# Late-token flag read two slots earlier, the common arm laid behind its branch, and the last slots of a mixture of experts reordered

## The chip, the core and the metric

The kernel runs on one core of a Trainium2 chip. The metric is the device time of one execution in microseconds. Of the kernel before, three runs took 663.84, 665.45 and 667.47 us (median 665.45). The profile comes from one further execution, of 667.0 us.

The core has five engines, each with its own queue of instructions, worked off in order: TensorE (PE, matmuls into PSUM; PEld is its weight load, listed apart), VectorE (DVE), ScalarE (ACT), GpSimd (POOL) and SyncE (SP, which here only issues DMAs). They wait for each other through semaphores.

## The reference

Three layers over 4 batches of 544 rows (32 global and 512 local) of 512 features, all in fp32:

```
x = attention(q_l, k_l, v_l, q_g, k_g, v_g)            # (4, 544, 512)
# layer 2: one expert of 8 for each row
logits = x @ w_gate; local = sigmoid(x @ w_local)
for s in rows of a batch:
    e = argmax(logits[s]) if s == 0 or local[s] < 0.5 else previous e
    y[s] = softmax(logits[s])[e] * (relu(x[s] @ w1[e]) @ w2[e])
# layer 3
h = relu(y @ w_in)
out = (h * sigmoid(conv3(h, conv_w))) @ w_out          # conv3 over the rows of a batch
```

The expert of a row depends on the data. `w_in`, `conv_w` and `w_out` of layer 3 arrive as 64-bit floats and are converted by integer operations on the chip.

## The kernel before, in words

**Products.** Each fp32 product is made of three matmuls in the type fp32r: every operand is split into a high part (a cast) and a low part (operand minus high part), and hi*hi, hi*lo and lo*hi are added up in PSUM. A weight's split is one ScalarE cast (`wh`, L1020) and one VectorE subtraction (`wl`, L1021).

**Slots.** Layer 2 gathers rows of one expert into slots of 128. Slots 0 and 1 are filled from the first rows while attention still runs. From slot 2 on (`Moe.run`, L1163) a `step` per slot goes through one straight line of code: first product of slot s (`l1`, 24 matmuls into `hp`), relu, transposes of the next slot's rows (`xs` to `xh`, `xl`), second product of slot s-1 (`l2`, 24 matmuls into `yp`), copy of `yp` to `ys` and scatter to `y_dram` by GpSimd, transposes of slot s's hidden rows (`hs` to `gh`, `gl`). So PE always has one product of each of two neighbouring slots. The straight line holds 22 slots, 0 to 21. Three more can be needed for other data; they stand in a conditional arm, the late arm.

**Weights of an expert.** W1 and W2 have one staging buffer each (`ws`). Where a slot has another expert than the one before, its splits run in a conditional arm on ScalarE and VectorE (`resplit`, L1268): W1's in the step before the slot, W2's at the end of the slot's own step.

**Beside the slots.** In steps 3 to 18 a chunk of `w_in` or `w_out` is loaded raw and converted (`conv64`, L983): six VectorE operations, one GpSimd addition, and a closing VectorE operation that is called in the next step. `wf` is their target. The conv weights (`cw6` to `cwr`, 24 x 128) are converted in the same way after step 19. `conv_w` (L1157) transposes `cwr` on PE and copies it to `cw`.

**Late tokens.** Layer 3 begins with batch 0. `late_tokens` (L924) marks whether a row of batch 0 sits in the last slot, and `late_flag` (L936) adds this mark, by a one-column matmul, to the test whether the late arm's slots are in use. All engines load the result from `esi` into a register and branch on it (L1172, L1173). If it is zero, nothing of the arm is done.

**The last slot, 21** (`last`, L1186): two of its four k parts of the first product, slot 20's second product, the other two parts with the conv weights and the flag among them, transposes, and its own second product. In that one lie layer 3's first pieces: the first batch's rows are loaded (`load0`), scaled by their gates one at a time (`scale0`), transposed (`xt0`, into `f_x0h`, `f_x0l`), and W1 is replaced by the split `w_in` (`split`). PREP0 lists what stands behind which k.

**Layer 3** (`Ffn2`) goes over 32 units of batch and feature block: 24 matmuls of 272 columns into `f1`, relu, three taps (one on ScalarE, two on VectorE), sigmoid, gate, split; then the second product. `w_out` is split at its beginning, on ScalarE and VectorE.

The program is recorded by hand: on each engine the instructions stand in the order in which the code calls them. At a conditional, an engine without instructions in an arm passes over it; an arm that isn't taken has a short partner that sets the semaphores to the values that the arm would have left.

Of the kernel before, what the change touches and what calls it, by code (L numbers as in the profile page):

```python
# [17 lines left out]
P = 128  # L18
# [6 lines left out]
NT = 17  # L25
# [940 lines left out]
SPLIT_W2 = {33: (0, 1), 34: (2, 3), 35: (4, 5), 36: (6, 7)}  # L966
FILL = {1: 1, 3: 1, 6: 3, 7: 1, 8: 3, 9: 1, 10: 1, 11: 1, 12: 2, 13: 3, 15: 5, 16: 8}
HALF = 5
K_LAST = 2
N_GLOB = 6  # L970
N_GS = 4
G_DVE = 1
N_Y = 24
SC_DVE = (0, 1, 2, 3)
PREP_F = ((3, 4, 5, 6), (1, 3, 5, 6), (1, 3, 5, 6))
PREP0 = {0: (0, 1, 12, 13), 3: (5, 2), 4: (6, 3), 5: (7, 4), 6: (8,), 7: (9,)}
POOL_L = ()
POOL_F = ()
DVE_F = (1, 3, 5, 7)
POOL_K = {1: (), 2: ()}  # L980


def conv64(nc, raw, out):  # L983
# [13 lines left out]
class Weights:  # L997
# [24 lines left out]

    def split(self, n, src, eng=None):
        for k in range(len(self.t[n])):
            self.split_k(n, src, k, eng or (self.nc.gpsimd if k in POOL_K[n] else self.nc.vector))


class Moe:
# [134 lines left out]
    def run(self, cw6, cwr, cw, f2):  # L1163
        nc, W, tc = self.nc, self.W, self.tc
        n = NSLOT - 3
        self.f2 = f2
        for s in range(NA, n - 1):
            self.step(s)
            if s == NA + 17:
                self.conv.append(conv64(nc, cw6, cwr))  # L1170
        self.last(n - 1, cwr, cw)
        r = nc.values_load(self.rt.esi[0:1, 4, 1:2], min_val=0, max_val=P + 1)  # L1172
        with tc.If(r != 0):  # L1173
            r = nc.values_load(self.rt.esi[0:1, 4, 0:1], min_val=0, max_val=NB)
            with tc.If(r > n - NA):
                for s in range(n, NSLOT):
                    self.slot(s)
                W.split(1, W.f)
            f2.load0()
            for i in range(5):  # L1180
                f2.scale0(i, self.ps)
                f2.xt0(i, self.ps)
        for k in range(NFC):
            W.split_k(2, W.f, k, nc.gpsimd if k in POOL_F else nc.vector, nc.vector if k in DVE_F else None)

    def last(self, s, cwr, cw):  # L1186
        nc, W, f2 = self.nc, self.W, self.f2
        hp, hs = self.h_tile(), self.tp.tile([P, FF], F32, tag="hs", name="hs")
        xt, ht = self.xt.pop(s), {}
        w, y = W.t[1], {}  # L1190
        ht = tuple(self.tp.tile([P, NFC, P], F32R, tag="g" + x, name="g" + x) for x in "hl")

        def split(a, b):
            for k in range(a, b):
                W.split_k(1, W.f, k, nc.gpsimd if k in POOL_K[1] else nc.vector)

        def resplit(a, b):
            with self.tc.If(self.chg[s] != 0):
                for k in range(a, b):
                    W.split_k(2, W.s, k, nc.gpsimd if k in POOL_L else nc.vector)  # L1200

        for k in range(K_LAST):
            self.l1_mm(xt, w, hp, k, range(2))
        split(0, K_LAST)
        nc.scalar.activation(self.sig, self.sig, AF.Sigmoid)
        self.out(s - 1, self.l2(self.ht.pop(s - 1), W.t[2]))
        f2.load0()
        resplit(0, 4)
        for k in range(K_LAST, NKC - 1):
            self.l1_mm(xt, w, hp, k, range(2))  # L1210
        self.conv_w(cwr, cw)
        self.rt.late_flag(s + 1, self.ps.tile([P, 4, P], F32, tag="tr", name="lf")[0:1, 0, 0:1])
        t = []
        for c in range(2):
            self.l1_mm(xt, w, hp, NKC - 1, (c,))
            self.relu_c(hp, hs, c)
        for a in (0, 4):
            t.append(self.hi_t(hs, ht, a, self.ps))
        for a in (0, 4):
            self.lo_t(ht, a, t[a // 4])  # L1220
        resplit(4, NFC)
        yp = self.y_tile()
        for k in range(NFC):
            self.l2_mm(ht, W.t[2], yp, k)
            for f in PREP0.get(k, ()):
                if f < 10:
                    (f2.scale0 if f < 5 else f2.xt0)(f % 5, self.ps)
                else:
                    split(f - 10, f - 9)
        self.out(s, yp)  # L1230

    def slot(self, s):
        nc, W = self.nc, self.W
# [37 lines left out]
        with self.tc.If(self.chg[s] != 0):  # L1271
            self.W.split(n, self.W.s, eng)

    def step(self, s):
        W, hi = self.W, NSLOT - 3
        if NA < s <= NA + 16:
            self.raw_load(s - NA - 1)
        hs = self.relu(self.l1(self.xt.pop(s), W.t[1]))
        if s + 3 < hi:
            self.xs[s + 3] = self.gather(s + 3)  # L1280
        self.xt[s + 1] = self.hi_lo_t(self.xs.pop(s + 1), NKC, "x")
        while self.conv:
            self.conv.pop()()
        self.resplit(s + 1, 1)
        if s + 2 < hi:
            self.fetch(s + 1, 1)
        if s == NA:
            for _ in self.rest:
                pass
        else:  # L1290
            self.out(s - 1, self.l2(self.ht.pop(s - 1), W.t[2]))
        self.ht[s] = self.hi_lo_t(hs, NFC, "g")
        self.resplit(s, 2)
        self.fetch(s, 2)
        if NA < s <= NA + 16:
            self.convert(s - NA - 1)
# [15 lines left out]
class Ffn2:  # L1312
# [14 lines left out]
    def part0(self, i):  # L1327
        return (SG, 0, GT, 4) if i == 0 else (P, SG + P * i - P, i - 1, i - 1)

    def scale0(self, i, ps):  # L1330
        n, _, j, a = self.part0(i)
        x = self.x_in[a][0:n]
        self.nc.vector.tensor_scalar(x, x, self.gate[0:n, j:j + 1], None, ALU.mult)
# [227 lines left out]
def moe_kernel(ctx, tc, q_l, k_l, v_l, q_g, k_g, v_g, w_gate, w_local, w1, w2, w_in, conv_w, w_out, out):  # L1561
    nc = tc.nc
    outf = out.rearrange("b s d -> (b s) d")
    with tc.manual_schedule():
# [95 lines left out]
        with ExitStack() as c2:  # L1660
# [15 lines left out]
            m.xt[NA] = m.hi_lo_t(m.xs.pop(NA), NKC, "x")  # L1676
            m.fetch(NA, 1)
            rt.gates()
            rt.late_tokens(NSLOT - 4)
        xa.close()  # L1680
        W.ffn(moe_ctx.enter_context(tc.tile_pool(name="w_f", bufs=1)))
        m.run(cw6, cwr, cw, f2)
# [34 lines left out]
```

## Time and profile before

| | |
|---|---|
| median of three runs | 665.45 us |
| profiled execution | 667.0 us, span 665.2 us, mean granted PE clock 0.968 |
| PE busy | 617.4 us (93%), 5898 matmuls |
| PEld busy | 517.8 us (78%) |
| VectorE busy | 421.7 us (63%) |
| ScalarE busy | 331.8 us (50%) |
| GpSimd busy | 199.0 us (30%) |

Times in the views are us from the span's start. Layer 2's straight line reaches from about 190 to 453 us, layer 3 from 457 us to the end. A timeline row gives start, duration from the first start to the last end of the merged instructions, engine, line of the code, operation, target and sources, shapes and count, and in brackets the idle time of the engine just before, with what ended it. Matmuls are pipelined: the distance from one start to the next tells their rate, the duration doesn't. [...] A queue's own instructions (loads of registers, branches, semaphores) have a "q" behind the engine's name; PE's stand under PEldq.

### The profile page before, as it was taken

What the parts mean: (1) busy time and instruction counts of PE and PEld (TensorE: products, weight loads), DVE (VectorE), ACT (ScalarE), POOL (GpSimd) and SP (SyncE); (2) the same over time, 40 slices, a digit from 0 to 9 for tenths busy, and PEclk for the clock granted to TensorE, in tenths of its full rate; (3) what the DMA queues carried; (4) which work ended last, traced back from release to release, by engine and by line L of the source; (5) the groups of instructions that cost most, each with busy time, mean ns of one, the idle gap of its engine ahead of it and who ended that gap; (6) DMA issues with size and microseconds to landing.
All of it is one profiled execution on the core that took longest, in us unless ns stands there. A gap on an engine that the chain in (4) does not pass through costs nothing. (4 is left out here: it accounts for less than half of the span.)

```text
span 665.2 us, 15266 instructions
## 1 busy us (share of the span) xinstructions
PE 617.4 (93%) x5898; PEld 517.8 (78%) x5898; DVE 421.7 (63%) x863; ACT 331.8 (50%) x634; POOL 199.0 (30%) x242
## 2 busy tenths in 40 slices
PE   7788797789789999999999999987989999999997
PEld 6576676566568888888888888866988898898886
DVE  7868576574773577776766697667985365373340
ACT  4745447956124444742554464663854364373341
POOL 7673810027331224323223223100365042300200
PEclk9989988798799999999999999997989999999999
DMA  8896853255028665466346565222010011000001
GB/s 223 202 250 167 233 123 72 95 191 189 0 66 285 237 222 184 165 247 221 88 185 225 204 233 210 85 84 85 1 47 33 33 64 48 17 17 33 33 33 47
DMA packets 59353, 86.05 MB, mean 129 GB/s; under 512 B 25358, under 2 KB 33830, under 8 KB 59240
## 3 DMA queue, kind: packets, MB, share of 16 engines
q1 hardware_dynamic: 55752, 74.77, 35.7%
q0 software_dynamic: 3520, 10.23, 4.5%
q8 instruction: 48, 0.79, 0.5%
q14 instruction: 33, 0.27, 0.1%
HBM read 125.87 MB, written 15.79 MB: 213 GB/s over the span
## 5 line engine op out<-in xcount | busy, mean ns | idle before, releaser
L1427 DVE SCALAR_TENSOR_TENSOR fc<-f_hp,cw,fc 128x544 f32<-128x544 f32 (+2 forms) x66 | 57.4, 870 | 70.7 <-ACT fc L1425 69.3
L1100 PE MATMUL yp<-wh,gh 128*128 128x512 f32 x176 | 71.7, 407 | 1.4 <-ACTq L1271 1.1
L1100 PE MATMUL yp<-wl,gh 128*128 128x512 f32 x176 | 69.4, 394 | 0.4 <-DVEq L1271 0.4
L1021 DVE TENSOR_TENSOR wl<-ws,wh 128x512 fp32r<-128x512 f32 (+1 forms) x84 | 66.7, 862 | 4.5 <-ACT wh L1020 4.4
L1100 PE MATMUL yp<-wh,gl 128*128 128x512 f32 x176 | 69.5, 395 | 0.0
L1020 ACT CAST wh<-ws 128x512 fp32r<-128x512 f32 (+1 forms) x96 | 66.1, 778 | 0.0
L1249 ACT ACTIVATE hs<-hp 128x512 f32<-128x512 f32 x44 | 24.3, 595 | 73.5 <-PE hp L1084 73.4
L1084 PE MATMUL hp<-wh,xh 128*128 128x512 f32 x176 | 58.9, 407 | 0.7 <-ACT xh L1073 0.7
L1084 PE MATMUL hp<-wl,xh 128*128 128x512 f32 x176 | 56.4, 393 | 0.0
L1084 PE MATMUL hp<-wh,xl 128*128 128x512 f32 x176 | 56.3, 392 | 0.0
L1485 PE MATMUL f<-wh,fh 128*128 128x512 f32 (+1 forms) x144 | 55.5, 385 | 0.0
L1057 POOL DMA_INDIRECT y_dram<-ys,sidx x22 | 25.7, 1169 | 97.9 <-ACT ys L1253 81.1
L1485 PE MATMUL f<-wl,fh 128*128 128x512 f32 (+1 forms) x144 | 55.0, 382 | 0.0
L1485 PE MATMUL f<-wh,fl 128*128 128x512 f32 (+1 forms) x144 | 55.0, 382 | 0.0
L993 POOL TENSOR_TENSOR wf<-wf,fx 128x512 int32<-128x512 int32 x16 | 20.9, 1306 | 99.5 <-DVE fx L992 99.5
L274 ACT ACTIVATE pr<-sp,nm 128x128 f32<-128x128 f32 x128 | 36.6, 377 | 28.1 <-DVE nm L271 28.1
L1077 DVE TENSOR_TENSOR gl<-hlp,gh 128x512 fp32r<-128x512 f32 x44 | 28.4, 685 | 32.4 <-ACT gh L1073 27.4
L1045 POOL DMA_INDIRECT xs<-x_dram,gidx x22 | 27.4, 1245 | 54.9 <-ACT pr L274 43.4
L1253 ACT COPY ys<-yp 128x512 f32<-128x512 f32 x22 | 12.9, 587 | 61.2 <-PE yp L1100 56.5
L1432 ACT ACTIVATE f_hp<-f 128x544 f32<-128x544 f32 x31 | 19.4, 627 | 42.4 <-PE f L1408 42.3
L1100 PEld LDWEIGHTS yp<-wh,gh 128*128 128x128 f32 x176 | 33.5, 190 | 8.0 <-ACTq L1271 1.4
L1084 PEld LDWEIGHTS hp<-wl,xh 128*128 128x128 f32 x176 | 33.1, 189 | 7.9 <-DVE wl L1021 0.9
(360 smaller groups left out, 1566.6 us busy)
## 6 DMA issues: line engine op xcount, KB each, us to landing
ws<-in_moe_w_dram SPq DMA_DIRECT2D x42, 2048.0 KB
fx<-y_dram SPq DMA_DIRECT2D x17, 256.0 KB
x_dram<-x SPq DMA_DIRECT2D x16, 256.0 KB
fx<-in_moe_w_in_dram SPq DMA_DIRECT2D x8, 512.0 KB
fx<-in_moe_w_out_dram SPq DMA_DIRECT2D x8, 512.0 KB
out_dram<-fy SPq DMA_DIRECT2D x16, 256.0 KB
VA<-in_v_l_dram SPq DMA_DIRECT2D x20, 192.0 KB
raw<-in_q_l_dram SPq DMA_DIRECT2D x3, 1024.0 KB
```

What stands on the lines that cost most here:

```text
L274: nc.scalar.activation(pr[:, hp, :], sp[:, hp, :], AF.Exp, bias=nm[:, hp:hp + 1], scale=-1.0)
L993: nc.gpsimd.tensor_tensor(a, a, lo, ALU.add)
L1020: (cp.tensor_copy if cp else self.nc.scalar.copy)(h, src[n][:, k, :])
L1021: eng.tensor_tensor(l, src[n][:, k, :], h.bitcast(F32), ALU.subtract)
L1045: self.nc.gpsimd.indirect_dma_start(out=xs, out_offset=None, in_=self.x_dram[0:n, :], in_offset=bass.IndirectOffsetOnAxis(ap=self.rt.gidx[ ...
L1057: self.nc.gpsimd.indirect_dma_start(out=self.y_dram[:, :], out_offset=bass.IndirectOffsetOnAxis(ap=self.rt.sidx[:, s:s + 1], axis=0), in_= ...
L1077: self.nc.vector.tensor_tensor(hl[1][:, a:a + 4], t, hl[0][:, a:a + 4].bitcast(F32), ALU.subtract)
L1084: self.nc.tensor.matmul(hp[c], a[:, k, :], b[:, 512 * c:512 * c + 512], start=k == 0 and m == 0, stop=k == NKC - 1 and m == 2)
L1100: self.nc.tensor.matmul(yp, a[:, k, :], b, start=k == 0 and m == 0, stop=k == NFC - 1 and m == 2)
L1249: self.nc.scalar.activation(hs[:, 512 * c:512 * c + 512], hp[c], AF.Relu)
L1427: nc.vector.scalar_tensor_tensor(c[:, a:b], hp[:, a + t:b + t], self.cw[:, t, f:f + 1], c[:, a:b], ALU.mult, ALU.add)
L1485: self.nc.tensor.matmul(yp[:, cs], x[:, c], w[:, cs], start=f == 0 and n == 0, stop=f == NFC - 1 and n == 2)
```

## The change

Five things change together.

1. The flag. `late_tokens` counts from slot 19 instead of 21. `conv_w`, `late_flag` and the register load by all engines move from the last slot and from behind it into step 19, between the fourth and fifth k part of slot 18's second product. The conv weights are converted after step 18, one step earlier.
2. The first batch's loads (`load0`) are issued ahead of step 20 instead of inside slot 21.
3. Slot 21 goes in the order of the others: its first product, slot 20's second, its own second. The five scales run at once ahead of it, the five `xt0` lie between its k parts.
4. The last product is copied into a piece of layer 3's input buffer (`x_in[3]`), and its scatter stands behind the branch, in the late arm and again in the common code.
5. The conditional names the false arm as the one to fall through to.

```diff
-K_LAST = 2
-PREP0 = {0: (0, 1, 12, 13), 3: (5, 2), 4: (6, 3), 5: (7, 4), 6: (8,), 7: (9,)}
+PREP0 = ((0, 1), (2,), (3,), (4,))
...
         for s in range(NA, n - 1):
-            self.step(s)
-            if s == NA + 17:
+            if s == n - 2:
+                f2.load0()
+            self.step(s, (cwr, cw) if s == NA + 17 else None)
+            if s == NA + 16:
                 self.conv.append(conv64(nc, cw6, cwr))
-        self.last(n - 1, cwr, cw)
-        r = nc.values_load(self.rt.esi[0:1, 4, 1:2], min_val=0, max_val=P + 1)
-        with tc.If(r != 0):
+        for i in range(5):
+            f2.scale0(i)
+        y = self.last(n - 1)
+        with tc.If(self.flag != 0, preferred_fallthrough_block=False):
+            self.scatter(n - 1, y)
+            nc.vector.memset(self.rt.sidx[:, n - 1:n], 4 * P * NT)
             r = nc.values_load(self.rt.esi[0:1, 4, 0:1], min_val=0, max_val=NB)
             with tc.If(r > n - NA):
...
             f2.load0()
             for i in range(5):
-                f2.scale0(i, self.ps)
+                f2.scale0(i)
                 f2.xt0(i, self.ps)
+        self.scatter(n - 1, y)
...
+    def last(self, s):
         nc, W, f2 = self.nc, self.W, self.f2
+        v = nc.vector
+        nc.scalar.activation(self.sig, self.sig, AF.Sigmoid)
+        xt, hp = self.xt.pop(s), self.h_tile()
+        for k in range(NKC):
+            self.l1_mm(xt, W.t[1], hp, k, range(2))
+            for i in PREP0[k]:
+                f2.xt0(i, self.ps)
+        hs = self.tp.tile([P, FF], F32, tag="hs", name="hs")
+        for c in range(2):
+            self.relu_c(hp, hs, c)
+        for k in range(2):
+            W.split_k(1, W.f, k, v)
         ht = tuple(self.tp.tile([P, NFC, P], F32R, tag="g" + x, name="g" + x) for x in "hl")
...
+        yp, hp = self.y_tile(), self.ht.pop(s - 1)
         for k in range(NFC):
+            self.l2_mm(hp, W.t[2], yp, k)
+            if k in (1, 2):
+                t = self.hi_t(hs, ht, 4 * k - 4, self.ps)
+                self.lo_t(ht, 4 * k - 4, t)
+        with self.tc.If(self.chg[s] != 0):
+            W.split(2, W.s, v)
+        self.out(s - 1, yp)
+        for k in range(2, NKC):
+            W.split_k(1, W.f, k, v)
+        yp = self.l2(ht, W.t[2])
+        y = f2.x_in[3]
+        nc.scalar.copy(y, yp)
+        return y
...
-            self.out(s - 1, self.l2(self.ht.pop(s - 1), W.t[2]))
+            yp, ht = self.y_tile(), self.ht.pop(s - 1)
+            for k in range(NFC):
+                self.l2_mm(ht, W.t[2], yp, k)
+                if k == 3 and cw:
+                    self.conv_w(*cw)
+                    self.rt.late_flag(hi, self.ps.tile([P, 4, P], F32, tag="tr", name="lf")[0:1, 0, 0:1])
+                    self.flag = self.nc.values_load(self.rt.esi[0:1, 4, 1:2], min_val=0, max_val=P + 1)
+            self.out(s - 1, yp)
...
-            rt.late_tokens(NSLOT - 4)
+            rt.late_tokens(NSLOT - 6)
```

The lines of the changed kernel are numbered otherwise (the second product's matmul is L1100 before and L1096 in the change). In the rows that follow, `wh2_3` is the high part of the fourth of W2's eight pieces, `gh` and `gl` are the hidden rows' parts.

On PE in step 19, in slot 18's second product, before:

```order
L1100 MATMUL yp_6634<-wh2_3_2726,gh_6514 128x512 [waits Activation_49]
L1100 MATMUL yp_6634<-wl2_3_2727,gh_6514 128x512 [waits DVE_49]
L1100 MATMUL yp_6634<-wh2_3_2726,gl_6515 128x512
L1100 MATMUL yp_6634<-wh2_4_2728,gh_6514 128x512 [waits Activation_49]
L1100 MATMUL yp_6634<-wl2_4_2729,gh_6514 128x512 [waits DVE_49]
L1100 MATMUL yp_6634<-wh2_4_2728,gl_6515 128x512
```

and in the change:

```order
L1096 MATMUL yp_6642<-wh2_3_2726,gh_6514 128x512 [waits Activation_49]
L1096 MATMUL yp_6642<-wl2_3_2727,gh_6514 128x512 [waits DVE_49]
L1096 MATMUL yp_6642<-wh2_3_2726,gl_6515 128x512
L1156 MATMUL cwp_6655<-ident_64,cwr_75 128x24 [waits DVE_49,PE_49]
L938 LDWEIGHTS late_87
L938 MATMUL lf_6658<-c_ones_1056,late_87 1x1 [waits PE_49]
L1258 UNCONDITIONAL_BRANCH
L1284 TENSOR_LOAD esi_83 [waits DVE_49,Pool_49]
L1096 MATMUL yp_6642<-wh2_4_2728,gh_6514 128x512 [waits Activation_49]
```

The transposes of the conv weights (`cwp`), the flag product (`lf`) and PE's load of the flag from `esi` now stand between the fourth and the fifth piece.

On VectorE behind step 18, from the last of the six operations that convert a chunk of `w_out` (`wf2`) to step 19, before:

```order
L992 TENSOR_SCALAR fx_3434<-fx_3434 128x512 [waits DVE_49]
L1077 TENSOR_TENSOR xl_6585<-hlp_6586,xh_6584 128x512 [waits Activation_49]
L994 SCALAR_TENSOR_TENSOR wf2_3948<-wf2_3948,fx_3434 128x512 [waits Pool_49]
L1264 TENSOR_LOAD esi_83
L1271 COMPARE_AND_BRANCH
```

and in the change:

```order
L988 TENSOR_SCALAR fx_3434<-fx_3434 128x512 [waits DVE_49]
L983 TENSOR_SCALAR cwr_75<-cw6_76 24x128
L984 SCALAR_TENSOR_TENSOR cwr_75<-cw6_76,cwr_75 24x128 [waits DVE_49]
L985 TENSOR_SCALAR cw6_76<-cw6_76 24x128 [waits DVE_49]
L986 TENSOR_SCALAR cw6_76<-cw6_76 24x128 [waits DVE_49]
L987 SCALAR_TENSOR_TENSOR cwr_75<-cw6_76,cwr_75 24x128
L988 TENSOR_SCALAR cw6_76<-cw6_76 24x128 [waits DVE_49]
L1073 TENSOR_TENSOR xl_6592<-hlp_6593,xh_6591 128x512 [waits Activation_49]
L990 SCALAR_TENSOR_TENSOR cwr_75<-cwr_75,cw6_76 24x128 [waits Pool_49]
L990 SCALAR_TENSOR_TENSOR wf2_3948<-wf2_3948,fx_3434 128x512
```

The six operations on the conv weights (`cwr`, `cw6`) now stand ahead of `xl`, the low part of slot 20's rows, and their closing operation ahead of the chunk's. A few rows further on VectorE in step 19, in the change only, behind the W1 split that isn't run there:

```order
L1258 UNCONDITIONAL_BRANCH [waits DVE_49]
L1157 COPY cw_77<-cwp_6655 128x24 [waits PE_49]
L939 TENSOR_SCALAR esi_83<-esi_83 1x1
L940 TENSOR_TENSOR esi_83<-lf_6658,esi_83 1x1 [waits DVE_49,PE_49]
L1284 TENSOR_LOAD esi_83 [waits DVE_49]
```

These are the copy of the transposed conv weights, the two operations on the flag, and VectorE's own load of it. Before, the copy and the flag stood in slot 21.

On PE at the end of layer 2, from the last matmuls of slot 21 to the first of layer 3 (`f1`), before:

```order
L1340 MATMUL f_tr0_7001<-ident_64,fx_3434 128x128 x3
L1172 TENSOR_LOAD esi_83 [waits DVE_49,Pool_49]
L1173 COMPARE_AND_BRANCH
L1174 TENSOR_LOAD esi_83
...
L1173 UNCONDITIONAL_BRANCH
L1173 UNCONDITIONAL_BRANCH [waits PE_49,PE_sequencer_49]
L1408 MATMUL f1_7506<-f_x0h_3435,wh1_0_2712 128x272 [waits Activation_49]
```

and in the change:

```order
L1096 MATMUL yp_6996<-wh2_7_2734,gl_6930 128x512
L1172 COMPARE_AND_BRANCH
L1172 UNCONDITIONAL_BRANCH [waits PE_49,PE_sequencer_49]
L1175 TENSOR_LOAD esi_83
...
L1172 UNCONDITIONAL_BRANCH
L1402 MATMUL f1_7508<-f_x0h_3435,wh1_0_2712 128x272 [waits Activation_49]
```

Before, the compare passes over the late arm to its partner, whose rows wait for PE's semaphores and which is directly followed by layer 3. In the change the partner stands directly behind the compare, and its branch passes over the late arm to layer 3.

## Rows read from the trace of the kernel before

**Rows 1.** PE's waits from 428 to 500 us: us in total, times, longest.
```profile
PE f L1408 <- PEq L1173: 3.9, 1, 3.9
PE f_tr L1373 <- DVE fxl L1375: 2.7, 1, 2.7
```

**Rows 2.** Line L1173, the branch: instruction, count, ns min/median/max, first and last start.
```profile
L1173 PEldq COMPARE_BRANCH  x1: 3528/3528/3528, 452.9 to 452.9; - x1
L1173 ACTq COMPARE_BRANCH  x1: 55/55/55, 453.3 to 453.3; - x1
```

**Rows 3.** Line L1172, the load of the flag into a register, on PE.
```profile
L1172 PEldq TENSOR_LOAD <-esi x1: 488/488/488, 452.3 to 452.3; - x1
```

**Rows 4.** DMA queues from 453 to 454 us: packets, MB, share of 16 engines.
```profile
q8 instruction: 1, 0.02, 6.8%
```

**Rows 5.** Timeline of PE, slots 18 to 21 and the start of layer 3.
```profile
412.73 0.39 PE L1100 MATMUL yp<-wh,gh 128*128 128x512 f32 x1
...
421.82 0.60 PE L1072 MATMUL hlp<-ident,xs 128*128 128x128 f32 x4
422.17 0.48 PE L1100 MATMUL yp<-wh,gh 128*128 128x512 f32 x1
...
427.74 1.03 PE L1072 MATMUL hlp<-ident,hs 128*128 128x128 f32 x8
428.54 0.72 PE L1084 MATMUL hp<-wh,xh 128*128 128x512 f32 x2
...
452.19 0.63 PE L1340 MATMUL f_tr<-ident,fx 128*128 128x128 f32 x4
456.75 0.56 PE L1408 MATMUL f<-f_x0h,wh 128*128 128x272 f32 x1 [3.93 <-PEq L1173]
```

**Rows 6.** Timeline of VectorE, steps 18 to 20.
```profile
405.71 4.89 DVE L1021 TENSOR_TENSOR wl<-ws,wh 128x512 fp32r<-128x512 f32 x8
...
413.23 0.43 DVE L992 TENSOR_SCALAR fx<-fx 128x512 int32<-128x512 int32 x1
...
415.08 0.69 DVE L994 SCALAR_TENSOR_TENSOR wf<-wf,fx 128x512 int32<-128x512 int32 x1 [0.83 <-POOL wf L993]
...
418.24 0.21 DVE L987 TENSOR_SCALAR cwr<-cw 24x128 int32<-24x128 int32 x1
...
424.05 0.27 DVE L994 SCALAR_TENSOR_TENSOR cwr<-cwr,cw 24x128 int32<-24x128 int32 x1
```

**Rows 7.** Timeline of GpSimd: the addition in the conversion of the conv weights.
```profile
419.81 0.45 POOL L993 TENSOR_TENSOR cwr<-cwr,cw 24x128 int32<-24x128 int32 x1 [2.25 <-DVE cw L992]
```

**Rows 8.** Timeline of VectorE in slot 21.
```profile
429.10 1.29 DVE L1077 TENSOR_TENSOR gl<-hlp,gh 128x512 fp32r<-128x512 f32 x2
...
440.58 0.18 DVE L1161 COPY cw<-cwp 128x24 f32<-128x24 f32 x1
...
440.91 0.15 DVE L940 TENSOR_TENSOR esi<-lf,esi 1x1 int32<-1x1 f32 x1
...
443.39 2.49 DVE L1021 TENSOR_TENSOR wl<-ws,wh 128x512 fp32r<-128x512 f32 x4
445.80 0.86 DVE L1333 TENSOR_SCALAR fx<-fx,gate 32x512 f32<-32x512 f32 x2
446.59 2.34 DVE L1021 TENSOR_TENSOR wl<-wf,wh 128x1024 fp32r<-128x1024 f32 x2
```

**Rows 9.** Stretches: length, busy time and instructions of PE, PEld, DVE, ACT, POOL, PEclk, DMA share, GB/s.
```profile
455.00:463.00 8.00, 6.25 (x29) 6.29 (x30) 5.62 (x11) 2.63 (x5) 0.44 (x7) 0.57 0.49 138
485.00:491.00 6.00, 5.87 (x35) 5.87 (x36) 5.07 (x7) 2.46 (x5) 2.25 (x3) 0.72 0.16 51
```

**Rows 10.** Timeline of ScalarE in slot 21.
```profile
439.59 1.24 ACT L1249 ACTIVATE hs<-hp 128x512 f32<-128x512 f32 x2
...
441.57 1.08 ACT L1073 CAST gh<-hlp 128x512 fp32r<-128x512 f32 x2 [0.73 <-PE hlp L1072]
...
444.61 2.00 ACT L1020 CAST wh<-wf 128x1024 fp32r<-128x1024 f32 x2
```

## What was predicted

> **What bounds the kernel now.** I read the waits of TensorE first. From 428 to 500 us there are two that matter: 3.9 us in front of the first matmul of the last stage, ended by PE's own sequencer at the late-token branch (L1173), and 2.7 us behind VectorE in that stage [rows 1]. Then the branch line: on PE one COMPARE_BRANCH took 3528 ns, on ScalarE the same jump 55 ns [rows 2]; the register load ahead of it took 488 ns on PE [rows 3]. In the microsecond from 453 on one packet of queue q8 moved, 0.02 MB of instructions [rows 4]: code was fetched while PE stood. Then PE's timeline: slot 20's second product runs without a gap from 422.17 to 427.74, its transposes to 428.54 [rows 5]. So up to 428.54 PE is full and every wait put into it there is paid in full; from 428.54 to the last transposes' end at 452.82 the last slot takes 24.3 us; then comes the branch, until 456.75 [rows 5].
>
> **Term 1, added: a wait in slot 19.** In the change, PE transposes the conv weights, makes the flag product and loads the flag into a register between k=3 and k=4 of slot 18's second product, which runs in slot 19. In the trace PE is at that place at 412.73 [rows 5]. The transposes need the converted weights `cwr`. On VectorE their conversion now stands behind that of a W2 chunk, whose sixth operation starts at 413.23 and takes 0.43, because slot 18's W2 split (4.89 us) was in front [rows 6]. So it starts at 413.7. Its six operations, up to GpSimd's add, took 1.6 us (418.24 to 419.81) [rows 6, 7]: add at 415.2, 0.45 long [rows 7], beside VectorE's `xl` subtraction. The closing operation (0.27 [rows 6]) ends at about 416.0 to 416.1. PE waits 3.4 us for it. Then VectorE has the W2 chunk's closing operation in front (0.69 [rows 6]), to 416.7, and copy and two flag operations, 440.58 to 441.06, 0.48 long [rows 8]: 417.2. PE's register load with what lies around it is 0.7 (0.49 [rows 3] and 0.1 on either side, estimated): PE goes on at 418.0. Term 1 is 418.0 - 412.73 = 5.3 us. Queued behind PE's load are all its matmuls, so nothing covers it; ScalarE, GpSimd and SP load the same register, but with slack in this slot. Bounds: 1.4 us, if `cwr` were ready (0.48 + 0.7 and the hop to VectorE), and 6.0, if the hops between engines are slower.
>
> **Term 2, added: the clock.** [...] I take the middle, 2.3; bounds 0 and 3.4.
>
> **Term 3, saved: the last slot.** PE's matmuls stay the same, and their order changes. Three products of 24 matmuls at 5.57 (slot 20's) make 16.7; transposes of `hs` 0.80; five groups of first-batch transposes at 0.35 (421.82 to 422.17) and an estimated 0.09 for each restart, 2.2 [rows 5]. Waits that stay: slot 20's `gl` ends at 430.4 on VectorE [rows 8], a scale takes 0.43 [rows 8], so the first transposes start at 431.0 while PE is there at 430.0 (a quarter of 5.57 after 428.54): 1.0. Ahead of the last product: first product and transposes end at 437.3, the last `x0` cast some 0.6 later; ScalarE then has two relus 1.24, two W1 casts 2.0 and two `gh` casts 1.08 [rows 10], and VectorE two W1 subtractions (2.34, from 440.2), two `gl` (1.29) and the first of eight W2 subtractions (2.49 for four) [rows 8]: 444.5. PE is there at 443.9: 0.6. The other seven follow 0.61 apart, while PE uses one in 0.68, so they don't bind. Sum: 428.54 + 16.7 + 0.8 + 2.2 + 1.0 + 0.6 = 449.85, against 452.82: 2.95 saved. Bounds: 4.55, if both new waits vanish, and 1.35, if they are twice as long.
>
> **Term 4, the branch.** The compare is no longer taken. But the common arm that is laid behind it is two semaphore instructions and an unconditional branch, and that branch passes over the same late arm, some 175 rows of the order, as the taken compare did. The semaphore instructions wait for PE's last matmul, so the jump can't start under it. The trace shows no far unconditional jump on PE; its price lies between 0.05 (ScalarE's jump) and 3.53 (PE's own) [rows 2]. I take PE's own: same engine, same distance, and the fetch of [rows 4] is of the target, which is no nearer. So of 3.93 only the register load goes and the compare comes on top: 0.1 saved; bounds 0 and 3.6.
> [...]
>
> **The rest** costs nothing: five scales run under PE's first product; the first-batch loads stand a whole slot ahead of their scales, behind slot 18's scatter; the last scatter follows the copy of the last product while PE jumps, as before, so the next batch's loads don't fall behind. ScalarE's and VectorE's W2 splits are released before PE's jump instead of after it, but the first tap waits for PE's first unit as before.
>
> **Sum.** 5.3 + 2.3 - 2.95 - 0.1 = +4.55. Against the profiled execution (667.0, span 665.2) that is 671.55. The median of the three runs shown, 665.45, lies 1.55 below, so the predicted time is 670.0. About 0.5%, 3.3 us, is what a measurement of this kernel can tell from no change.
>
> **Rivals.**
> The jump is free: the place is PE's unconditional branch, the price 0.05 in place of 3.53. For it: 55 ns on ScalarE [rows 2], and a target that is known beforehand. Against it: the same distance. It gives +4.55 - 3.5 = +1.05, and a little less, since the last stage's first unit would run at the higher clock, most of which VectorE's lateness [rows 1] takes back: 666.2. [...]
> The clock holds in slot 19: the small products in the middle of the wait keep it up. Against it: both waits shown, one of 2.7 us only, lowered it. +4.55 - 2.3 = +2.25: 667.7.
> Not slower: `cwr` is ready when PE asks. It decides from the point where its closing operation ends before 412.7, 3.3 us earlier than I have it; then term 1 is 1.4, term 2 is 0 and the sum 1.4 - 3.05 = -1.65, 663.8; with the free jump on top 660.3. Against it stands slot 18's W2 split on VectorE, 405.71 to 410.6 [rows 6].
> The late arm runs: the threshold now counts first-batch rows in slots 19 and 20 too. If one is there, loads, scales and transposes come a second time: in series five times 0.43 + 0.35 = 3.9 [rows 5, 8], a far jump more or less, 3.5, and the loads on top, over 8 in all, near 679. Against it: W2 is split in slot 18 and not again in 19 or 20 [rows 6], so these hold the later rows of one expert, and the reference's inputs give that expert four first-batch rows, which rank first, in slot 18.
>
> **How the numbers follow.** Forecast 0.62, free jump 0.14, clock holds 0.12, weights ready 0.09, late arm 0.03. The forecast's own range is 668.5 to 672.0 (terms 1 and 2 from 4.8 + 1.7 to 5.6 + 3.4, terms 3 and 4 together at 3.05, some 0.4 either way). The range 664.3 to 673.0 takes in the free jump and the clock that holds. Slower by over 0.5%: 0.64 (nearly all of the forecast, and the late arm). Within 0.5%: 0.28 (free jump, clock, part of the weights). Faster: 0.08 (weights ready together with a free jump, or a last slot that saves far more).
>
> **What would show it.** In the profile after: PE idle between the fourth and fifth part of slot 18's second product, ended by VectorE's conversion and then by PE's own register load, 5 us together; a granted clock of half behind it; a COMPARE_BRANCH on PE of some 3.5 us at the late-token line with a q8 packet in it; 21.3 us from the first matmul of slot 21 to the end of its last. A branch of 0.1 us, or a wait under 2 us in slot 19, would make the prediction wrong.

## The result, and the profile after

The change makes the kernel slower: 672.64 us median of seven runs against 666.04 us of seven of the kernel before; the ratio is 1.0077 (95% interval 1.0052 to 1.0102). The forecast was 670.0 us, +4.55 on the profiled execution. The measured time lies 0.6 above the forecast's own range (668.5 to 672.0) and inside the wide one (664.3 to 673.0). The medians differ by 6.6 us, with an interval of 3.5 to 6.8, so the forecast was on the low side. The execution profiled after took 672.64 us with a span of 670.9, 5.7 above the span before.

Where the 5.7 us lie is read by cutting both timelines at the same points of the program:

| stretch | before | after | difference | forecast |
|---|---|---|---|---|
| to the transposes of slot 18's hidden rows | 403.16 | 401.98 | -1.2 | 0 |
| from there to those of slot 20 (steps 19, 20) | 24.58 | 33.57 | +9.0 | +7.6 |
| from there to layer 2's last matmul's end | 25.08 | 22.16 | -2.9 | -2.95 |
| from there to layer 3's first matmul | 3.93 | 3.73 | -0.2 | -0.1 |
| layer 3 to the end of the span | 208.45 | 209.46 | +1.0 | 0 |

The first line is ahead of everything changed here, and nearly all of its difference stands already at the transposes of slot 2's hidden rows (205.77 before, 204.65 after). At the end of this stretch the fourteen profiled executions of this study lie between 401.98 and 409.14 us, so a single span says little about an edit, and the later stretches, each from its own start, say more.

PE's waits in the kernel after, as [rows 1]: us in total, times, longest.

```profile
PE cwp L1156 <- DVE cwr L990: 4.2, 1, 4.2
PE f L1402 <- ACT wh L1016: 3.7, 1, 3.7
PE f_tr L1367 <- DVE fxl L1369: 3.7, 2, 3.0
PE yp L1096 <- DVE esi L940: 1.5, 1, 1.5
PE f_tr L1334 <- DVE fx L1327: 1.0, 1, 1.0
```

The first and the fourth row are the new wait in slot 19: for the conv weights, then for the flag. The third is layer 3's wait for VectorE, 2.7 before; the last is the one for the first scale in slot 21. The second is the wait at the branch, which the profile now puts down to a cast of ScalarE that had long ended; the queue's rows show what it is, as [rows 2]:

```profile
L1172 PEldq COMPARE_BRANCH  x2: 90/1712/3334, 456.4 to 458.0; - x2
L1172 PEldq EVENT_SEMAPHORE  x2: 51/51/51, 457.8 to 457.9; - x2
```

Two branches: the compare that is not taken, 90 ns at 456.4, and the unconditional one behind the two semaphore instructions, 3334 ns at 458.0. PE's timeline answers to [rows 5]; between the two last rows the branch stands.

```profile
411.32 0.39 PE L1096 MATMUL yp<-wh,gl 128*128 128x512 f32 x1
415.93 0.21 PE L1156 MATMUL cwp<-ident,cwr 24*128 24x24 f32 x1 [4.22 <-DVE cwr L990]
416.06 0.16 PE L938 MATMUL lf<-c_ones,late 128*1 128x1 bf16 x1
417.71 0.76 PE L1096 MATMUL yp<-wh,gh 128*128 128x512 f32 x1 [1.48 <-DVE esi L940]
418.27 0.63 PE L1096 MATMUL yp<-wl,gh 128*128 128x512 f32 x1
418.70 0.63 PE L1096 MATMUL yp<-wh,gl 128*128 128x512 f32 x1
...
435.55 1.03 PE L1068 MATMUL hlp<-ident,hs 128*128 128x128 f32 x8
...
457.32 0.39 PE L1096 MATMUL yp<-wh,gl 128*128 128x512 f32 x1
461.44 0.59 PE L1402 MATMUL f<-f_x0h,wh 128*128 128x272 f32 x1 [3.73 <-ACT wh L1016]
```

Without the wait the fifth piece would start at 411.55, 0.23 behind the matmul before it; it starts at 417.71. Behind it matmuls follow 0.43 us apart and not 0.23. The two stretches (columns as [rows 9]): the gap, and the second half of the product with the granted clock at 0.54 (0.50 up to 423.5, 1.00 from 424.1 on).

```profile
411.50:417.70 6.20, 0.51 (x3) 0.23 (x3) 5.09 (x14) 0.00 (x0) 1.73 (x2) 0.93 0.86 320
417.70:424.10 6.40, 6.39 (x21) 5.13 (x21) 0.00 (x0) 0.77 (x2) 0.00 (x0) 0.54 0.00 0
```

VectorE in that gap, as [rows 6]: the order is the one forecast, but the second operation on the conv weights takes 1.35 us (0.28 before). The last row is GpSimd's addition for the chunk, which runs beside it.

```profile
412.39 0.21 DVE L983 TENSOR_SCALAR cwr<-cw 24x128 int32<-24x128 int32 x1
412.64 1.35 DVE L984 SCALAR_TENSOR_TENSOR cwr<-cw,cwr 24x128 int32<-24x128 int32 x1
...
415.50 0.28 DVE L990 SCALAR_TENSOR_TENSOR cwr<-cwr,cw 24x128 int32<-24x128 int32 x1
415.71 0.67 DVE L990 SCALAR_TENSOR_TENSOR wf<-wf,fx 128x512 int32<-128x512 int32 x1
416.53 0.18 DVE L1157 COPY cw<-cwp 128x24 f32<-128x24 f32 x1
```

```profile
412.57 1.28 POOL L989 TENSOR_TENSOR wf<-wf,fx 128x512 int32<-128x512 int32 x1 [8.48 <-DVE fx L988]
```

And what nobody had forecast, around layer 3's start. ScalarE's copy of slot 20's product behind its casts of W2, GpSimd's last two scatters, SyncE's loads of the second batch, VectorE's first scale of them:

```profile
449.74 4.29 ACT L1016 CAST wh<-ws 128x512 fp32r<-128x512 f32 x8
453.91 0.61 ACT L1240 COPY ys<-yp 128x512 f32<-128x512 f32 x1
```

```profile
454.80 4.68 POOL L1053 DMA_INDIRECT y_dram<-ys,sidx  x1 [17.12 <-POOLq L1172]
463.04 1.29 POOL L1053 DMA_INDIRECT y_dram<-fx,sidx  x1 [3.56 <-DVE wl L1017]
```

```profile
465.79 3.51 SPq L1352 DMA_DIRECT2D fx<-y_dram  x5
```

```profile
467.67 1.68 DVE L1421 SCALAR_TENSOR_TENSOR fc<-f_hp,cw,fc 128x544 f32<-128x544 f32 x2 [1.45 <-ACT fc L1419]
472.44 0.49 DVE L1360 TENSOR_SCALAR fx<-fx,gate 128x512 f32<-128x512 f32 x1 [3.09 <-DMA fx<-y_dram]
```

The loads start 4.35 us behind layer 3's first matmul (before: 457.08, 0.3 behind it), and VectorE stands 3.09 us in the middle of its taps.

### The profile page after: what moved, and what is told of

Same layout as the page of the kernel before. It is cut to its first block, busy times and chain, and to the rows that moved or that the text cites. A ratio compares the mean times of both kernels' runs of the same rounds, so it can differ in the third digit from the quotient of the medians.

```text
span 670.9 us, 15265 instructions
## 1 busy us (share of the span) xinstructions
PE 617.9 (92%) x5898; PEld 519.1 (77%) x5898; DVE 423.1 (63%) x863; ACT 331.1 (49%) x634; POOL 202.9 (30%) x242
## 5 line engine op out<-in xcount | busy, mean ns | idle before, releaser
L1096 PE MATMUL yp<-wh,gh 128*128 128x512 f32 x176 | 73.7, 419 | 2.6 <-DVE esi L940 1.5
L1096 PE MATMUL yp<-wl,gh 128*128 128x512 f32 x176 | 71.5, 406 | 0.6 <-DVEq L1258 0.4
L1096 PE MATMUL yp<-wh,gl 128*128 128x512 f32 x176 | 71.4, 405 | 0.0
L1053 POOL DMA_INDIRECT y_dram<-ys,sidx x21 | 27.5, 1309 | 101.2 <-ACT ys L1240 82.5
L1096 PEld LDWEIGHTS yp<-wh,gh 128*128 128x128 f32 x176 | 34.5, 196 | 9.5 <-issue 1.5
L1096 PEld LDWEIGHTS yp<-wl,gh 128*128 128x128 f32 x176 | 34.7, 197 | 8.0 <-DVEq L1258 0.7
```

The costliest lines, as they stand in the source:

```text
L1053: self.nc.gpsimd.indirect_dma_start(out=self.y_dram[:, :], out_offset=bass.IndirectOffsetOnAxis(ap=self.rt.sidx[:, s:s + 1], axis=0), in_= ...
L1096: self.nc.tensor.matmul(yp, a[:, k, :], b, start=k == 0 and m == 0, stop=k == NFC - 1 and m == 2)
```

## The experiments

Each ratio is to the kernel before, run in turn with it; the change's own is 1.0077. "Stand" is PE's idle time from layer 2's last matmul's end to layer 3's first matmul (before 3.93 us, after 3.73); "rest" is from the same point to the end of the span (before 212.4 us, after 213.2). The expectations put the end of the last product 0.16 us earlier than the profile does, so that their stand of 3.9 in the change is 3.7 here. Numbers of stages are of one profiled execution each.

**1. Without the wait in slot 19.**

```diff
-            if s == NA + 16:
+            if s == NA + 15:
                 self.conv.append(conv64(nc, cw6, cwr))
...
-            self.step(s, (cwr, cw) if s == NA + 17 else None)
+            self.step(s, (cwr, cw) if s == n - 2 else None)
...
 # step 20, first product:
+            if k == 1 and cw:
+                t = self.conv_w(*cw)
+                self.rt.late_flag(hi, t[0:1, 1, 0:1])
...
 # slot 21, first product:
+            if k == 0:
+                self.flag = nc.values_load(self.rt.esi[0:1, 4, 1:2], min_val=0, max_val=P + 1)
```

The three calls in step 19's second product go.

> The change, but the conv weights are converted one step earlier, transposed and the flag computed inside slot 20's first product, and the register load stands in slot 21 behind the first k part, where PE waits 1.0 us anyway. Theory (the stall in slot 19 is the loss): PE's 6.2 us gap and the half clock behind it (12 matmuls at 0.43 instead of 0.23 us, transposes 0.3 longer) go together, 9.0 us; 0.2 come back for the two small products; the time is about 8.5 us under the changed kernel's, 1.3% of it, which is some 3 us under the kernel before: ratio to it 0.995 (0.992 to 0.998). Rival (the clock would fall anyway, from later waits): only the gap goes, 6.0 us, ratio 0.999. Rival (another engine is as late in slot 19): ratio above 1.003.

665.86 us, ratio 0.9978 (0.9951 to 1.0004). The two steps, 19 and 20:

```profile
403.00:415.30 12.30, 12.30 (x62) 10.23 (x61) 10.71 (x20) 7.28 (x14) 3.84 (x3) 1.00 0.43 145
415.30:428.40 13.10, 12.83 (x63) 10.36 (x62) 6.03 (x10) 6.92 (x10) 1.00 (x1) 1.00 0.51 179
```

PE is all but full and the clock is 1.00 throughout: 25.4 us against 33.6 in the change and 24.6 before. So 8.2 us of the 9.0 that the change loses here were this wait and the clock behind it; the rest is the two small products and a wait of 0.3 us behind the first. By the ratios the gain over the change is 0.99%, 6.6 us, less than the 8.5 expected; the two intervals together leave 4 to 9. Against the kernel before the gain is not settled by this run: the rival's 0.999 lies in the interval too, but the clock of 1.00 speaks against the rival.

**2, 4 and 5. The jump.** The second run lets the compare be taken again and asks for its target ahead:

```diff
-        with tc.If(self.flag != 0, preferred_fallthrough_block=False):
+        with tc.If(self.flag != 0, label="late"):
...
-        yp = self.l2(ht, W.t[2])
+        with self.tc.block():
+            self.tc.mark_branch_hint_location("late", "LikelyTaken", [mybir.EngineType.PE])
+            yp = self.l2(ht, W.t[2])
```

> The change with the compare taken again (the late arm behind it, the common arm behind that) and, ahead of the last product, a branch prefetch hint on PE that names this compare. Theory (the jump's price is the fetch of its target): PE's stand between the last matmul of slot 21 and layer 3's first falls from 3.9 us to under 0.6, with the instruction packet 3 to 6 us earlier. Theory on the rest (layer 3's VectorE chain starts from the second batch's rows, which land at 472.4 whatever PE does): the end moves by less than 1 us, ratio to the kernel before 1.006 to 1.008, and VectorE's wait for the rows grows from 3.1 to over 5 us. Rival (PE's jump is on the path to the end): ratio 1.002 to 1.003. Rival (the jump costs 3.3 us in itself): the stand stays at 3.5 or more.

673.47 us, ratio 1.0082 (1.0051 to 1.0113). The hint on PE, the compare, taken over the same late arm, and VectorE's first scale in layer 3:

```profile
L1708 PEldq BRANCH_PREFETCH_HINT  x1: 45/45/45, 454.4 to 454.4; - x1
```

```profile
L1172 PEldq COMPARE_BRANCH  x1: 388/388/388, 462.9 to 462.9; - x1
```

```profile
478.56 0.49 DVE L1362 TENSOR_SCALAR fx<-fx,gate 128x512 f32<-128x512 f32 x1 [4.29 <-DMA fx<-y_dram]
```

388 ns instead of 3334; the packet of queue q8 moved at 455.33, behind the hint and 7.6 us ahead of the compare; the stand is 0.77 us instead of 3.73. The end got little of these 3 us: PE's waits for VectorE in layer 3 add up to 7.1 us instead of 3.7, and the rest is 212.6, 0.6 less. Both theories held in kind. Their numbers were partly missed: the stand did not fall under 0.6, the wait for the rows grew to 4.3 us and not over 5, and the ratio lies just above 1.008.

The fourth run keeps the change's layout and takes the three late slots out of the arm:

```diff
             nc.vector.memset(self.rt.sidx[:, n - 1:n], 4 * P * NT)
-            r = nc.values_load(self.rt.esi[0:1, 4, 0:1], min_val=0, max_val=NB)
-            with tc.If(r > n - NA):
-                for s in range(n, NSLOT):
-                    self.slot(s)
-                W.split(1, W.f)
```

> The change without the three late slots in the late arm (left out: the slots 22 to 24, which these inputs do not use), so that PE's unconditional branch passes over some 50 instructions instead of 410. Theory (the price is the distance: the target's block has not been fetched): the branch falls from 3.33 us to under 0.3 and the stand to 0.7, with no instruction packet inside it; the end as with the target fetched ahead, ratio 1.006 to 1.008. Rival (an unconditional branch on PE costs 3.3 us by itself, or by draining the engine): the stand stays at 3.9 us.

672.35 us, ratio 1.0069 (1.0037 to 1.0102).

```profile
L1172 PEldq COMPARE_BRANCH  x2: 90/202/313, 456.8 to 458.2; - x2
L1172 PEldq EVENT_SEMAPHORE  x1: 51/51/51, 458.1 to 458.1; - x1
```

The unconditional branch takes 313 ns, the stand is 0.77 us, and no instruction packet moves between 455 and 459. So neither the branch itself nor draining the engine costs 3.3 us. Again the end gains nothing (rest 213.2); VectorE waits 5.2 us for the rows.

The fifth is the change with `tc.If(self.flag != 0)` and nothing else.

> The change with the compare taken, as before it: the late arm behind the compare, its partner and layer 3 behind the arm; nothing fetched ahead. One look. Theory (the jump can run under PE's last matmuls if no semaphore instruction stands ahead of it): the compare starts about 1.1 us before the last product's end, takes 3.3 to 3.5 us, and the stand is 2.7 us instead of 3.9; with the rows of the second batch late anyway the span stays within 2 us of the changed kernel's once the stage ahead is equal: from the last product's end to the end 213 to 214 us. Rival (the layout is not what the stand hangs on): 3.9 us.

One run, the profiled one, with a span of 669.1 us:

```profile
L1172 PEldq COMPARE_BRANCH  x1: 3477/3477/3477, 456.1 to 456.1; - x1
```

The compare starts at 456.1, 1.3 us ahead of the last matmul's end (457.33), runs under it, and the stand is 2.5 us; the rest is 211.8, under the 213 expected. So laying the common arm directly behind the branch costs 1.2 us of PE here: its two semaphore instructions, which wait for the last matmul, stand ahead of the far jump. A single run doesn't tell whether the end gains.

**3. The rows scaled later.**

```diff
-                if b + 1 < B and f < 4:
-                    x2[b + 1, f] = self.scaled(...)
+                i = f - (2 if b == 0 else 0)
+                if b + 1 < B and 0 <= i < 4:
+                    x2[b + 1, i] = self.scaled(...)
```

> The change, but in layer 3 VectorE scales the second batch's row pieces two units later (units 2 to 5 instead of 0 to 3), so that its taps do not stand behind a load. Theory (the rows' late landing costs in layer 3): VectorE's 3.1 us wait goes, PE's 3.7 us of waits for VectorE in layer 3 fall under 1.5, and the time falls by 2 to 4 us: ratio to the kernel before 1.002 to 1.005. Rival (VectorE's chain is bound by its own work and the wait is slack): under 0.7 us, ratio 1.006 to 1.008.

673.68 us, ratio 1.0106 (1.0069 to 1.0144): the theory missed.

```profile
PE f_tr L1367 <- DVE fx L1360: 3.7, 2, 2.1
```

VectorE's wait for the rows is gone, but PE's transposes now wait 3.7 us for the scales, which stand behind the taps of two more units. A wait was moved, not removed.

**6. Slot 20's scatter out of VectorE's way.** With the target fetched ahead as above, and in slot 21:

```diff
             for i in PREP0[k]:
                 f2.xt0(i, self.ps)
+            if k in (1, 2):
+                W.split_k(1, W.f, k - 1, v)
...
-        for k in range(2):
+        for k in range(2, NKC):
             W.split_k(1, W.f, k, v)
...
         self.out(s - 1, yp)
-        for k in range(2, NKC):
-            W.split_k(1, W.f, k, v)
```

> The change with the target fetched ahead, as in the run on that, and with w_in's four pieces split earlier in slot 21: two inside its first product, two behind its relus, none behind W2's split. So ScalarE and VectorE are done sooner, slot 20's scatter meets no long run of VectorE, and the last scatter need not wait for it. Theory (a free jump is worth nothing while the second batch's rows land late): slot 20's scatter takes under 1.5 us on GpSimd instead of 4.68, the last scatter starts under 2 us behind the last product's end instead of 5.5, VectorE's wait for rows falls from 4.3 to under 1.5 us, and the time falls 2 to 4 us below the changed kernel's: ratio to the kernel before 1.0015 to 1.005. Rival (VectorE's own work binds layer 3's start): ratio 1.006 to 1.009 with VectorE's wait for rows gone all the same.

672.93 us, ratio 1.0074 (1.0042 to 1.0106).

```profile
455.43 2.41 POOL L1053 DMA_INDIRECT y_dram<-ys,sidx  x1 [17.13 <-ACT ys L1242]
461.75 1.38 POOL L1053 DMA_INDIRECT y_dram<-fx,sidx  x1 [3.91 <-DVE wl L1017]
```

The scatter falls from 4.68 to 2.41 us and the last one starts 3.4 us behind the last product, not under 2; VectorE still waits 4.4 us for the rows. The theory named the wrong link: the scatters are part of the lateness, but not what decides.

**7 and 8. All together, then with work taken from VectorE.** Run 7 is runs 1 and 6 in one kernel; run 8 adds `DVE_F = ()` and the scaling of run 3, one unit later instead of two.

> The kernel without the wait in slot 19 (as in the first run) with the target fetched ahead and w_in's pieces split earlier. Theory: the gain over the first run is the one that the run on the scatter shows over the changed kernel, 2 to 4 us: ratio 0.991 to 0.995. Rival (VectorE's own work binds): 0.997 to 0.999.

664.61 us, ratio 0.9963 (0.9932 to 0.9994), between the two theories, with a wait for rows of 4.1 us. It is not clear of run 1's 0.9978.

> The same, and two edits that take work from VectorE's start of layer 3: all eight casts of w_out on ScalarE (four were VectorE's, 0.42 us each), and the second batch's pieces scaled one unit later. Theory (VectorE's queue is what layer 3's start waits for once the rows are in time): another 1 to 2 us, ratio 0.988 to 0.993. Rival (ScalarE becomes late with the casts): no gain over the one before, ratio 0.991 to 0.997.

661.44 us, ratio 0.9923 (0.9895 to 0.9952). That is in the theory's range and in the rival's as well, and 0.40% below run 7 is within the noise of two such ratios; the rest, 209.2 us against run 7's 211.4, speaks for the theory. 3.2 us of the wait for rows stay.

**9 and 10. The pieces loaded first.** In run 2 the first piece's load has sixteen parts that complete one by one. By the trace's completion records twelve land at 474.6 to 475.3, and four at 477.9 to 478.5, when VectorE goes on. Ahead of it in SyncE's queue stands the load of the global rows, 4 times 32 rows, which completes in four parts only (477.2 to 478.1). The kernel before has the same split, twelve at 460.2 to 460.9 and four at 463.3 to 463.8, but there VectorE comes to the scale only at 465.69. So:

```diff
-                    if n == 0:
-                        xs["g"] = self.load_glob()
...
                         xs[b + 1, f] = self.load_x(b + 1, f)
+                    if n == 3:
+                        xs["g"] = self.load_glob()
```

> The change with the target fetched ahead, and in layer 3 the load of the global rows (32 rows of each batch, not needed before the fifth unit) issued behind the four loads of the second batch's pieces instead of ahead of them. In the run with the fetched target alone twelve of the first piece's sixteen parts land 4.0 us ahead of VectorE's scale, and four land 3 us later, with those of the global rows. Theory (that load ahead makes the first piece late, and the late piece hides the free jump): the four parts land with the twelve, VectorE's wait for rows falls from 4.3 to under 1.8 us, PE's waits for VectorE in layer 3 fall from 7.1 to about 4.5, and the time falls by 2 to 3 us below the changed kernel's: ratio to the kernel before 1.003 to 1.0055. Rival (VectorE's own work binds anyway): 1.006 to 1.009 with the wait gone.

670.24 us, ratio 1.0055 (1.0025 to 1.0085).

```profile
467.98 1.68 DVE L1423 SCALAR_TENSOR_TENSOR fc<-f_hp,cw,fc 128x544 f32<-128x544 f32 x2
469.58 0.48 DVE L1362 TENSOR_SCALAR fx<-fx,gate 128x512 f32<-128x512 f32 x1
```

All sixteen parts land within 469.0 to 469.4 and the scale follows the taps without a gap; PE's waits for VectorE in layer 3 fall from 7.1 to 3.9 us, and the rest is 208.4 us instead of 212.6. By the traces that is where the free jump had gone. The ratio, 0.27% below run 2's and 0.22% below the change's, is at the expectation's upper edge; the intervals overlap, so the time alone does not show the gain.

Why the load of the global rows completes in four parts and that of a piece in sixteen, no run shows. What the traces show is that four of the piece's parts land with it while it stands ahead (477.9 to 478.5 beside 477.2 to 478.1), and with the other twelve once it is issued behind the pieces.

> The kernel of the run with relief for VectorE (no wait in slot 19, target fetched ahead, w_in's pieces split earlier, w_out's casts on ScalarE, second batch's pieces scaled one unit later), and the global rows loaded behind the pieces. Theory: VectorE's 3.2 us wait for rows goes, PE's 5.0 us of waits for VectorE fall to about 2, and the time falls another 2 to 3 us: ratio to the kernel before 0.987 to 0.990. Rival (ScalarE or VectorE's own work is late next): no gain, 0.991 to 0.994.

659.70 us, ratio 0.9878 (0.9847 to 0.9909): faster than the kernel before by 1.2%, and than the change by 2.0%. PE's largest wait in layer 3 is now

```profile
PE f_tr L1374 <- DVE fxl L1376: 3.1, 1, 3.1
```

and it is VectorE's own work: from 459.42 until PE goes on at 477.78 VectorE has next to no idle time (busy 9.81 us of the 10 from 460 and 9.89 of the 10 from 470). PE's waits for VectorE were expected to fall to about 2.

**11. Dummies in the wait.** 18 matmuls of 512 columns ahead of the conv weights' transposes, 4 behind the flag product (`self.warm(18)`, `self.warm(4)`).

> The change with 18 matmuls of 512 columns, whose result nobody reads, on PE ahead of the conv weights' transposes in slot 19, and 4 more behind the flag product: work of 0.23 us each that fills most of PE's two waits (4.2 and 1.5 us) and no more. Theory (the half clock behind the wait is a consequence of the idle engine, and worth 2.8 us by the matmuls' spacing): the granted clock stays at 1.00 behind the wait, the twelve matmuls of the second half are 0.23 us apart instead of 0.43, and the time falls by 2.5 to 3 us below the changed kernel's: ratio to the kernel before 1.0025 to 1.0045. Rival (the clock falls for another reason, or the matmuls delay the load): 1.007 or more, spacing 0.43.

670.18 us, ratio 1.0044 (1.0021 to 1.0066). The gap is as long as before; the clock is not what it was:

```profile
413.30:419.50 6.20, 5.71 (x25) 4.08 (x23) 5.10 (x14) 0.00 (x0) 1.76 (x2) 1.00 0.86 318
419.50:423.20 3.70, 3.65 (x21) 3.11 (x21) 0.00 (x0) 0.55 (x2) 0.00 (x0) 1.00 0.02 4
```

Twelve matmuls and eight transposes take 3.7 us instead of 6.4. So the half clock of the change (0.54 over this half of the product, 1.00 here) came with the idle engine, and cost 2.7 of the 9.0 us. The time fell by 0.33%, 2.2 us, at the upper edge of what was expected. This kernel had a second effect that wasn't meant (last section), worth nothing at the end by runs 2 and 4.

**12. The weights ready, alone.** The first two lines of run 1's diff.

> The change with the conv weights converted one step earlier, and nothing else, so that they are ready when PE asks in slot 19; the copy, the flag and PE's register load stay there. The prediction's case of ready weights gave 1.4 us for the wait that stays, and the full clock: by it the time falls 7.5 us below the changed kernel's, ratio 0.996. Theory now (VectorE, not the weights, is late: behind W2's split it still has the raw chunk's conversion, which it ends 3 us after PE arrives): PE's gap falls from 6.2 to between 3.5 and 4.5 us and the clock still falls behind it; the time falls 2 us, ratio 1.003 to 1.006.

675.42 us, ratio 1.0101 (1.0067 to 1.0135). PE's waits in slot 19:

```profile
PE yp L1096 <- DVE esi L940: 2.6, 1, 2.6
PE lf L938 <- DVE xl L1073: 1.3, 1, 1.3
```

The gap is 4.3 us, as expected: VectorE comes to the flag (419.57) only behind W2's split (to 414.18) and the raw chunk (to 419.32). The clock still falls behind it, to 0.71 over 420.65 to 425.60. Steps 19 and 20 take 30.4 us (406.74 to 437.10), 3.2 less than in the change. The time does not show it and missed the expectation. The profiled execution is 4.8 us late already at the first point of the table, nearly all of it (4.7) at the transposes of slot 2, far ahead of the edit, and has 1.5 us more in the rest; why this kernel's runs lie so is open.

## Why the prediction was right, point by point

- **Bound.** PE full up to slot 21, so that a wait in slot 19 is paid in full: right. Run 1 without it gives 8.2 us back in these steps.
- **Term 1**, 5.3 us: measured 6.2 (411.55 to 417.71), above its upper bound of 6.0. The mechanism was as written, VectorE's order and then PE's register load. What was mis-sized is the conversion of the conv weights. Its second operation took 1.35 us, where [rows 6] had the six take 1.6 together, with GpSimd's addition for the chunk beside it (412.57 to 413.85). In the profiles of all thirteen kernels with this order the two lie side by side and it takes 1.34 to 1.38 us; before, the two never met and it took 0.28. That the addition is the reason is read from these pairs; no run moved it alone. PE also came 1.2 us earlier in this execution, and so did VectorE.
- **Term 2**, 2.3 us: measured 2.8 by the spacing (6.36 us from 417.71 to the next product at 424.07, 3.51 before), 2.7 by run 11, inside its bounds. No run shows what the 2.3 is the middle of. The traces show a granted clock of 0.50 for 6.8 us behind the 3.9 us wait of the kernel before and for 3.4 us behind its 2.7 us one; in the change it is at 0.50 from 417.7 to 423.5, behind the wait in slot 19, where matmuls of 512 columns stand 0.43 us apart and not 0.23.
- **Term 3**, 2.95 saved: 2.9. Its wait for the first scale was 1.0 us, as written.
- **Term 4**, 0.1 saved: 0.2. The price taken, PE's own 3.53, was right (3.33), and so was the reason that the target has to be fetched: the change's packet moves inside the jump (458.94), and runs 2 and 4 make it 0.39 and 0.31, with the packet 7.6 us ahead of it and with none from 455 to 459. That it had to be fetched here was in part luck: "same distance" does not decide it, since run 11 pays 0.31 over the same arm.
- **The rest, "the next batch's loads don't fall behind"**: wrong, and not priced. The last scatter does not follow the copy; it waits until slot 20's has landed at 462, which stood behind W2's casts on ScalarE (to 454.03) and took 4.68 us on GpSimd (the last three before: 0.97 to 1.03). The loads start 4.35 us after layer 3 instead of 0.3. Layer 3 is 1.0 us longer, and so are PE's waits for VectorE there (3.7 against 2.7). In the profiled sum the early part of this execution, 1.2 us shorter and not the change's doing, hid it: without that luck the 5.7 would be 6.9. The medians' 6.6 bear that out.
- **Rivals.** A free jump was refuted in price where the branch stands here (3.33 us). It would also not have given its 3.5 us: run 2 has it and gains 0.6 in the rest, since the second batch's rows are late anyway. The prediction priced it as if the end moved with PE's start of layer 3. The clock that holds: refuted (0.54). Weights ready: run 12 shows that 1.4 us was too little for what stays, since VectorE is late with or without them; 4.3 stay, and the clock falls all the same. The late arm did not run.

## What to carry to other kernels

A flag or a weight that PE needs early costs what the engine that makes it has queued in front of it, and the half clock behind the wait on top (here 6.2 us of wait and 2.7 of clock at 0.54): move the making and the reading apart by a whole step, as run 1 does. A jump made free, or any wait removed, is worth only what the next late thing leaves; find that one first (here four of sixteen parts of a load), by the wait that grows when the first goes. Which arm is laid behind a branch does not tell which arm is cheap: look for what waits ahead of the jump (1.2 us in run 5) and for whether the target's instructions are there (3.33 us in the change, 0.31 to 0.39 in runs 2, 4 and 11).

## What the runs showed of the hardware

- PE's jump over the late arm took 3.31 to 3.71 us in the kernel before, the change and runs 1, 3, 5 and 12; in the first two an instruction packet moves inside it (453.82 and 458.94). It took 0.39 us in runs 2, 6, 7 and 8, 0.31 in run 11, and 0.31 over the shorter arm of run 4; in run 4 no packet moves from 455 to 459, in runs 2 and 11 one moved 7.6 and 9.6 us ahead of the jump. It isn't the distance alone. In run 11 the 22 dummies shift PE's program by 42 instructions, and the change's own unconditional branch over the same late arm falls to 310 ns:

```profile
L1172 PEldq COMPARE_BRANCH  x2: 90/200/310, 455.6 to 457.2; - x2
```

  An instruction packet moved at 447.57, 9.6 us ahead of it; in the change none moves between 427.66 and the jump's own at 458.94. That the branch's place in the program is the reason is an inference from this one pair of kernels (3.33 us in the change, 0.31 in run 11); how far it must be shifted wasn't tried.
- With a prefetch hint of 45 ns, 8.5 us ahead of the compare, the jump took 0.39 us in place of 3.33 (run 2, and 0.77 us of stand in runs 6 to 10 as well). Run 2's packet moved about 1 us behind the hint (455.33, the hint at 454.4). The change has no hint, and its packet moved only inside the jump (458.94, the jump from 458.0 on).
- Slot 20's indirect scatter, which GpSimd begins within a run of VectorE's subtractions, ended 0.83 to 0.85 us behind that run, however long the rest of it was: 4.68 us in the change (the run ends at 458.65), 2.41 in runs 6 and 8. Others took 1.0 us beside such subtractions (1.03 us at 436.65 in the change, 0.97 at 437.89 before), so what decides is open.
